# An RWKV-5 layer with a feed-forward part: V loaded and cast by GpSimd's DMA queue, and a new order of steps

## The chip, the cores and the metric

The kernel runs on one core of a Trainium2 chip. The metric is the device time of one execution in microseconds, as the median of several runs. TensorE (PE) multiplies matrices, VectorE (DVE), ScalarE (ACT) and GpSimd (POOL) do elementwise work, SyncE (SP) issues DMAs; SP and GpSimd each have a DMA queue here. Each engine works through its own list of instructions in order and waits on semaphores for what it needs from others.

## The reference

Inputs are `r`, `k`, `v` of shape (4, 8, 768, 48) (batch, heads, time, head size), `w` and `u` of shape (8, 48), and the two matrices `w_in` (384 x 2048) and `w_out` (2048 x 384), all float32.

```python
for t in range(S):
    kt, vt, rt = k[:, :, t], v[:, :, t], r[:, :, t]
    cur = np.einsum('bhd,bhe->bhde', u[None] * kt, vt)
    y[:, :, t] = np.einsum('bhd,bhde->bhe', rt, state + cur)
    state = w[None, :, :, None] * state + np.einsum('bhd,bhe->bhde', kt, vt)
x = y.transpose(0, 2, 1, 3).reshape(B * S, H * D)        # 3072 x 384
h = x @ w_in
g = np.where(h >= 1, h, np.where(h <= -1, 0.0, (h + 1) ** 2 / 4))
return g @ w_out
```

## The kernel before, in words

The recurrence is computed in chunks of 128 time steps. There are six chunks and four batches; a **group** is one chunk of two batches (two **units**), so there are 12 groups, numbered 0 to 11, even ones for batches 0 and 1, odd ones for batches 2 and 3. A group holds 256 tokens.

For each group the kernel does this; the step's name in the order list is in brackets, and `g` stands for the group, `n = 2g + j` for a unit.

- Loads of R, K and V, time on the partitions, 16 heads of 48 values each (`LRg`, `LKg`, `LVg`). One load of a group is 384 KB in runs of 192 bytes. All three are issued on SP's queue. V arrives as float32 in `Vi`, and ScalarE casts it into the bfloat16 tile `Vb` (step `Vg`, L110 by way of the helper `copy`).
- R and K scaled by powers of w, in bfloat16 (`Rsg`, `Ksg`), K times u (`KUg`), R times that (`RKUg`), its sum over each head (`usg`, tile `diag`), and V times that sum (`Bg`, L295). These are products on GpSimd or VectorE; the letter behind "=" says which.
- Rs and Ks turned so that the head size lies on the partitions: by TensorE for the first three groups (`TR`, `TK`, `T`), by transposing DMAs on SP's queue from group 3 on (`RTg`, `KTg`).
- K^T R for each head (`An`, `AAg` for both units), masked to the upper triangle by VectorE (`ATn`). Y is the masked product times V plus the turned R times the state of the chunk before (`Yn`). `yg` adds B. K^T V (`Spn`) updates the state: `Tmg` on VectorE, `decayg` (tile `state`, L398), and a bfloat16 copy by ScalarE (`sbfg`).
- y is turned, by TensorE for groups 0 to 2 (`X`, `xc`), by a transposing DMA on SP's queue from group 3 on (`xcgg`, tile `xT`).
- The feed-forward part in four quarters q of 512 columns: `mg.q` (tile `hp`, 12 matmuls, L457), `rg.q` and `sg.q` on ScalarE (tiles `pt` and `sq`, L468 and L477), `gg.q` on VectorE (L480), `Mg.jq` for the token halves j (tile `op`, 4 matmuls, L492), then a copy out of PSUM (`ogg`) and the store on SP's queue (`stgg`).

The weights are loaded and cast to bfloat16 by DMAs on GpSimd's queue: w_in in three parts (`WI0`, `WI1`, `WI2`), w_out in two (`WO0`, `WO1`). `Zn` are n idle matmuls. Groups 0 and 1 are done by halves: in `LV1.0` the number behind the dot is the unit.

The order of all steps of all engines is one list written out by hand, `ORDER`. The program goes through it word by word, and each engine gets its instructions in that order. `SLOTS` gives the number of buffers of each tile: `Vi` has 3, `Vb` 4.

Of the kernel before, what the change touches and what calls it, by code (L numbers as in the profile page):

```python
# [25 lines left out]
Rs0.0=V WdnS Sp0/0 LK1.0 LK1.1 uS=A KU0.0=V KU0.1=G RKU0.1=G wE TR0/3 cK0=V cR0=A LR1.1 V0.1 wC=V Tm0 Rs0.1=V LV1.0  # L26
LV1.1 RKU0.0=V us0.0 Z16 A0/10 WI0 AT0.0 Ks1.0=G WI1 us0.1 B0.1=G B0.0=V LK2 TR1/2 cR1=A Z21 Sp1/1 AT0.1 Rs1.1=G Tm1
LR2 TK1/3 cK1=A Ks1.1=G TK2/2 Z11 A1/03 AT1.1 Z8 TR3/1 WI2 cR3=A Y0/3 AT1.0 y0 Z7 TK3/1 X0/3 KU1.1=V Rs1.0=V cK3=A
Y1/0 y1 Z14 X1/1 cK2=V V1.0 LK3 RKU1.1=V us1.1 xc0=A xc1=A TR2/2 A3/03 AT3.1 KU1.0=G cR2=A AT3.0 LV2 m0.1/1 r0.1=A
# [11 lines left out]
yg5 M3.03 og3=V xcg5 r4.1 m4.2/3 m4.3/1 g4.0 M4.00/2 M4.10 LK10 Ks7=G RT6 s4.1=A r4.2 LR8 g4.1 M4.01 M4.11 KU7=G  # L41
RKU7=G s4.2=A r4.3 LR10 g4.2 M4.02 M4.12 AA6/30 decayg4=G s4.3=A g4.3 Rs7=G RT7 us7 RKU6=G sbfg4=A m5.1/1 r5.1 M4.03
stg2 AT13 LV10 s5.1=A m5.0/0 r5.0 s5.0=A KU10=G LK8 AT12 KT7 Rs10=G us6 g5.1 M4.13 m5.3/3 Y12/1 Y13 og4=V r5.3 s5.3=A
B6=G g5.0 m5.2/2 r5.2 s5.2=A yg6 xcg6 Rs8=G g5.3 LK9 M5.00/0 Sp10/1 Sp11 M5.01 LR9 V7 Tmg5 decayg5=G M5.10 M5.11 stg4
AA7/31 stg3 g5.2 AT15 V10 m6.1/2 sbfg5=A r6.1 B7=G M5.02 RKU10=G RT8 AT14 m6.0/1 M5.03 m6.3/3 s6.1=A g6.1 KU8=G r6.0
s6.0=A Y14/2 Y15 Ks8=G M5.12 M5.13 r6.3 yg7 m6.2/2 xcg7 g6.0 s6.3=A KT8 og5=A LV11 g6.3 Sp12/1 Sp13 M6.00/0 M6.10
M6.01 M6.11 r6.2 RKU8=G Tmg6 LV8 m7.1/3 s6.2=A g6.2 decayg6=G sbfg6=A Rs9=G us10 AA8/12 r7.1 s7.1=A us8 M6.12 M6.13
LV9 M6.02 AT17 m7.0/2 LK11 AT16 Ks9=G KT9 g7.1 RT9 V8 B8=G Sp14/1 Sp15 M6.03 Tmg7 Y16/3 Y17 yg8 r7.0 s7.0=A m7.2/1
decayg7=G m7.3/3 stg5 Ks10=G r7.2 g7.0 M7.00/2 M7.01 M7.10 M7.11 s7.2=A g7.2 M7.12 xcg8 RT10 og6=V AA9/10 stg6 r7.3
s7.3=A V11 M7.02 LR11 g7.3 M7.03 m8.0/3 M7.13 AT18 KT10 Sp16/1 Sp17 sbfg7=A AT19 KU9=G RKU9=G V9 B10=G KU11=G r8.0  # L50
s8.0=A m8.1/0 us9 B9=G og7=V Y18/2 Y19 Tmg8 decayg8=G stg7 r8.1 s8.1=A g8.0 m8.2/1 m8.3/3 r8.2 Ks11=G yg9 xcg9 M8.00/2
M8.10 g8.1 M8.01 M8.11 s8.2=A Rs11=G KT11 g8.2 m9.0/0 r8.3 s8.3=A M8.12 g8.3 AA10/13 sbfg8=A r9.0 M8.02 M8.03 AT20
M8.13 m9.1/1 RKU11=G s9.0=A AT21 og8=A stg8 Sp18/3 Sp19 Y20/2 Y21 r9.1 s9.1=A g9.0 m9.2/0 RT11 yg10 xcg10 m9.3/2 g9.1
r9.2 M9.00/1 M9.10 M9.11 M9.01 s9.2=A r9.3 s9.3=A Tmg9 m10.0/3 decayg9=G g9.2 M9.02 g9.3 us11 B11=G AA11/20 AT23 M9.12
M9.13 M9.03 m10.1/0 AT22 sbfg9=A r10.0 s10.0=A og9=A stg9 r10.1 Y22/2 Y23 s10.1=A g10.0 M10.00/3 M10.10 m10.2/1 yg11
xcg11 m10.3/2 r10.2 s10.2=A g10.1 M10.11 M10.01 m11.0/0 r10.3 s10.3=A g10.2 M10.02 r11.0 M10.12 m11.1/1 g10.3 M10.03
s11.0=A g11.0 m11.2/2 r11.1 s11.1=A m11.3/0 M10.13 g11.1 M11.00/1 M11.01 r11.2 s11.2=A og10=V r11.3 s11.3=A stg10
M11.10/3 M11.11 g11.2 M11.02 M11.12 g11.3 M11.13 M11.03 o11.1=A st11.1 o11.0=A st11.0
# [14 lines left out]
def kernel(  # L73
# [169 lines left out]
    def do_WO(e, b, i):  # L243
        nc.gpsimd.dma_start(out=w_out_sb[i], in_=w_out_src[:, sum(OUT_PARTS[:i]) * FG : sum(OUT_PARTS[: i + 1]) * FG, :])


    def load(x, what, cls, g, j):
        j0, j1 = by_unit(g, j)
# [1 line left out]
        nc.sync.dma_start(out=t[:, j0 * H : j1 * H, :], in_=source(x, g, j0, j1))  # L250
# [309 lines left out]
```

## Time and profile before

| | |
|---|---|
| median of 3 runs | 182.53 us (180.95 to 185.12) |
| the profiled execution | 181.74 us, of which the span from the first to the last instruction is 180.0 us |
| mean granted TensorE clock | 0.991 |
| busy: TensorE, VectorE, ScalarE, GpSimd | 166.0, 134.7, 126.1, 114.5 us |
| first matmul of the feed-forward part | 20.01 us after the start of the span |
| last matmul ends, last store issued | about 176.4 us |
| DMA packets | 107,191, of which 100,898 are under 512 bytes |

The busy share of an engine is an average over the span; which engine sets the end is read from the stretch in question and from the wait that ends last there. In rows of the profile, a line such as "L110 ACT CAST Vb<-Vi 128x768 bf16<-128x768 f32 x10" names the line of the program, the engine, the operation, the output and input tiles with their shapes and types, and the count; behind the bar stand the total and mean time, and then the idle time of the engine before these instructions with what ended it. "SPq" is an issue on SP's queue. Queue q1 is SP's, q0 GpSimd's.

### The profile page before, as it was taken

How to read it: one execution, taken by the hardware profiler on the slowest of the kernel's cores; microseconds unless marked ns; L12 is line 12 of the kernel's file. 1: busy time of each engine (PE TensorE's matmuls, PEld its weight loads, DVE VectorE, ACT ScalarE, POOL GpSimd, SP SyncE). 2: the span in 40 equal slices, each digit the busy share in tenths (PEclk: the TensorE clock that was granted, in tenths of full speed). 3: DMA queues.
4: the chain of work that ended last, by engine and by line, in shares of the span. 5: the costliest groups of instructions: out<-in, count | busy, mean ns of one | idle time of the engine just before them, and what ended most of it. 6: DMA issues, size and time to landing. Idle time of an engine off the chain costs nothing.

```text
span 180.0 us, 4051 instructions
## 1 busy us (share of the span) xinstructions
PE 166.0 (92%) x1678; PEld 125.7 (70%) x1678; DVE 134.7 (75%) x156; ACT 126.1 (70%) x144; POOL 114.5 (64%) x82
## 2 busy tenths in 40 slices
...
GB/s 113 192 181 207 224 184 198 206 211 173 152 185 181 222 166 206 182 169 190 197 153 238 176 252 181 179 169 221 241 192 135 12 146 44 4 133 0 5 87 87
DMA packets 107191, 28.78 MB, mean 160 GB/s; under 512 B 100898, under 2 KB 106788, under 8 KB 107172
## 3 DMA queue, kind: packets, MB, share of 16 engines
q1 hardware_dynamic: 103888, 25.37, 80.0%
...
q14 instruction: 6, 0.05, 0.1%
q10 hardware_dynamic: 4, 0.00, 0.0%
...
## 4 chain that ended last, share of the span: by engine, by line
PE 65%; DMA 19%; DVE 5%; POOL 3%; SPq 3%; ACT 2%; issue 1%; DVEq 0%
PE op L492 29%; PE hp L457 28%; DMA w_out<-in_moe_w_out_dram 6%; DMA w_in<-in_moe_w_in_dram 4%; DMA xT<-y 4%; SPq L250 3%; DMA Ki<-in_k_dram 3%; DVE g L480 2%; PE A L352 2%; DMA out_dram<-o 2%; PE Y L420 2%; PE Y L414 2%; DVE y L432 2%; POOL Ks L264 2%; PE Sp L387 1%
## 5 line engine op out<-in xcount | busy, mean ns | idle before, releaser
L457 PE MATMUL hp<-xT,w_in 128*128 128x256 bf16 x576 | 70.5, 275 | 5.5 <-DMA xT<-y 3.6
L480 DVE SCALAR_TENSOR_TENSOR g<-sq,hp 128x1024 bf16<-128x1024 bf16 x48 | 58.2, 1217 | 17.4 <-ACT sq L477 17.1
L492 PE MATMUL op<-w_out,g 128*128 128x384 bf16 x384 | 69.0, 326 | 1.5 <-DMA w_out<-in_moe_w_out_dram 1.5
L457 PEld LDWEIGHTS <-w_in 128*128 128x128 bf16 x576 | 55.8, 98 | 16.2 <-DMA xT<-y 4.0
L468 ACT ACTIVATE pt<-hp 128x1024 f32<-128x1024 f32 x47 | 47.8, 1017 | 23.4 <-PE hp L457 23.3
L492 PEld LDWEIGHTS <-g 128*128 128x128 bf16 x384 | 36.2, 98 | 22.8 <-issue 1.4
L477 ACT ACTIVATE sq<-pt 128x1024 bf16<-128x1024 f32 x47 | 49.7, 1057 | 1.4
L295 POOL TENSOR_TENSOR V<-Vb,diag 128x768 f32<-128x768 bf16 (+1 forms) x13 | 17.3, 1329 | 16.0 <-ACT Vb L110 10.6
L361 DVE TENSOR_TENSOR AT<-A,umask 128x1024 bf16<-128x1024 f32 x20 | 23.6, 1218 | 3.5 <-PE A L352 3.5
L264 POOL TENSOR_TENSOR KU<-Ki,u_sb 128x768 f32<-128x768 f32 (+1 forms) x12 | 21.0, 1750 | 5.4 <-ACT u_sb L110 5.2
L398 POOL TENSOR_TENSOR state<-Tm,wCm 128x768 f32<-128x768 f32 x8 | 14.5, 1817 | 11.8 <-DVE Tm L395 11.8
L264 POOL TENSOR_TENSOR Ks<-Ki,Wdn 128x768 bf16<-128x768 f32 (+1 forms) x12 | 20.2, 1682 | 1.5 <-DMA Ki<-in_k_dram 1.5
L264 POOL TENSOR_TENSOR RKU<-Ri,KU 128x768 f32<-128x768 f32 (+1 forms) x12 | 20.3, 1696 | 0.7 <-DMA Ri<-in_r_dram 0.3
L264 POOL TENSOR_TENSOR Rs<-Ri,Wup 128x768 bf16<-128x768 f32 (+1 forms) x10 | 17.4, 1739 | 4.8 <-DMA Ri<-in_r_dram 4.8
L432 DVE TENSOR_TENSOR y<-Y,V 128x768 bf16<-128x768 f32 x10 | 9.6, 956 | 9.4 <-POOL KU L264 5.0
L110 ACT CAST state_bf<-state 128x768 bf16<-128x768 f32 (+1 forms) x12 | 8.6, 716 | 4.4 <-POOL state L398 4.4
L286 DVE TENSOR_REDUCE diag<-RKU 128x16 f32<-128x768 f32 (+1 forms) x14 | 11.6, 831 | 0.1
L110 ACT CAST Vb<-Vi 128x768 bf16<-128x768 f32 (+1 forms) x14 | 10.1, 734 | 1.8 <-DMA Vi<-in_v_dram 1.8
L420 PE MATMUL Y<-Vb,AT 128*128 128x48 bf16 x192 | 10.4, 187 | 0.7 <-ACT Vb L110 0.7
L110 ACT COPY o<-op 128x768 f32<-128x768 f32 (+1 forms) x7 | 4.9, 703 | 8.0 <-PE op L492 8.0
L420 PEld LDWEIGHTS <-AT 128*128 128x128 bf16 x192 | 9.6, 99 | 1.1 <-issue 0.9
L519 PE MATMUL z<-idle 128*128 128x128 bf16 x96 | 8.3, 253 | 1.2 <-DVE idle L132 1.2
...
## 6 DMA issues: line engine op xcount, KB each, us to landing
...
w_out<-in_moe_w_out_dram POOLq DMA_DIRECT2D x2, 768.0 KB, 9.5
...
```

Of the source, the lines that this page charges most:

```text
L110: nc.scalar.copy(out, in_) if e == "A" else engines[e].tensor_copy(out, in_)
L264: engines[e].tensor_mul(part(out)[:, :, :, :D], part(a), rep(b, j1 - j0) if len(b.shape) == 3 and b.shape[1] == H else part(b))
L295: engines[e].tensor_mul(t[:, hs, :], tiles["V", g][:, hs, :], tiles["diag", g][:, hs].unsqueeze(2).to_broadcast([P, n, D]))
L361: nc.vector.tensor_mul(t.rearrange("p i n t -> p (i n) t"), tiles["A", n].rearrange("p i (n t) -> p (i n) t", t=P), umask.unsqueeze(1).to_ ...
L398: engines[e].tensor_mul(states[g % BP], tiles["Tm", g], flat(wCm).unsqueeze(1).to_broadcast([P, UNITS, DM]))
L420: nc.tensor.matmul(Y[:, h * D : (h + 1) * D], AT[:, i, p, :], V[:, j * H + h, :], start=(c == 0), stop=True, skip_group_check=True,)
L432: nc.vector.tensor_add(y, tiles["Y", "of", g][:, :, :DM], flat(tiles["V2", g]).rearrange("p (j d) -> p j d", j=UNITS))
L457: nc.tensor.matmul(hp[:, f, :], w_in_sb[wi][:, i, (wo * FG + f) * P : (wo * FG + f + 1) * P], tiles["xT", g][:, :, i, :], start=(i == 0), ...
L468: nc.scalar.activation(t, tiles["hp", g, q], AF.Relu, bias=0.5, scale=0.5)
L477: nc.scalar.activation(t, p, AF.Square)
L480: nc.vector.scalar_tensor_tensor(out=make("g", ("g", g, q), [P, FG, TOK], BF16), in0=tiles["sq", g, q], scalar=1.0, in1=tiles["hp", g, q], ...
L492: nc.tensor.matmul(tiles[key][:, k, :DO], tiles["g", g, q][:, f, j * P : (j + 1) * P], w_out_sb[wi][:, wo * FG + f, :], start=(q == 0 and ...
```

## The change

`LVg` no longer loads float32 on SP's queue. It issues a DMA on GpSimd's queue that writes bfloat16 straight into `Vb`. The switch `CAST_FROM` is 0, so this holds for every group. The steps `Vg` are gone from the list, and the whole list is laid out anew. Some products move between GpSimd and VectorE: RKU2, RKU3, B3 and decay2 go to VectorE, and among the half steps of groups 0 and 1 some go each way.

```diff
 ORDER = """
-Zs/0 LV0.0 LK0.0 LK0.1 LR0.0 ln Z19 bw/0 V0.0 LV0.1 bu/1 LR0.1 Wdn/2 Ks0.1=V wq/3 WupS Ks0.0=V TK0/2 LR1.0 Wup/1
...
-s0.0=A sbf0=A g0.0 xc2=V Sp3/0 r0.2=A X3/1 xc3=V LR3 WO0 sbf1=A m0.3/0 Ks2=G s0.2=A Tm3 r0.3=A s0.3=A Rs2=G WO1 m1.1/2
...
-Y6/2 g2.0 KU4=G RKU4=G s2.1=A Y7 yg3 r2.2=A m2.3/1 RT4 M2.00/2 g2.1 Sp4/3 KU5=G s2.2=A r2.3=A s2.3=A xcg3 LR5 Sp5
...
-s3.0=A r3.1 s3.1=A M2.13 M2.03 LK6 g3.0 og2=A B4=G m3.2/3 Tmg3 LR6 RT5 sbfg2=A r3.2 s3.2=A LV5 AA4/20 g3.1 LK7 RKU5=G
-M3.00/1 M3.01 AT9 AT8 m3.3/0 Y8/2 g3.2 Ks6=G V6 Y9 yg4 xcg4 r3.3 M3.10 M3.11 s3.3=A AA5/32 us5 LR7 M3.02 KT6 M3.12
-g3.3 KU6=G decayg3=G sbfg3=A Rs6=G V5 AT11 Sp8/0 Sp9 M3.13 B5=G m4.0/2 stg1 AT10 Y10/3 Y11 Tmg4 LV7 m4.1/0 r4.0 s4.0=A
...
+Zs/0 LR0.0 LK1.0 ln LK0.0 LV0.0 Z20 bw/1 LK0.1 LV0.1 LR0.1 LV1.0 LR1.0 bu/3 WdnS Ks1.0=G WupS Wdn/0 uS=A wq/2 Wup/1
+LR1.1 Ks0.0=V KU0.0=V wE Ks0.1=V KU0.1=G wC=A LK1.1 Z7 TK1/1 TK0/3 cK1=A LV1.1 Rs0.1=V Z6 TR1/2 RKU0.0=V us0.0 LR2 WI0
+cR1=A Rs0.0=V LK2 Z17 TR0/1 LK3 A1/02 RKU0.1=V Rs1.0=G cR0=V cK0=V us0.1 AT1.1 B0.0=G Z14 Sp2/1 Z2 A0/23 Tm2 WI1
...
+AT3.1 AT2.0 us1.0 Sp3/3 AT3.0 B1.0=G r0.1=A m0.0/0 us1.1 WO0 s0.1=A Sp0/2 B1.1=G Y2/1 Tm0 g0.1 Y3/2 r0.0=A y2 m0.3/1
+s0.0=A y3 X3/0 r0.3=A s0.3=A g0.0 LR4 Ks2=G X2/2 xc2=V xc3=V m0.2/0 Tm3 g0.3 r0.2=A m1.1/2 m1.0/3 WO1 Rs2=V s0.2=A
...
+xc5=V us3 B3=V AA3/02 LV4 og1=A m2.0/1 RT4 sbf3=A AT6 KU4=G m2.1/3 sbf2=A r2.0=A s2.0=A Ks4=G AT7 m2.2/0 LK6 r2.1=A
+g2.0 s2.1=A Y6/2 Y7 M2.00/1 yg3 RKU4=G r2.2=A M2.10 g2.1 xcg3 m2.3/2 s2.2=A KU5=G KT4 M2.01 g2.2 r2.3=A Sp4/3 LR5 Sp5
+M2.11 M2.12 Ks5=G Tmg2 s2.3=A us4 LR6 LR7 m3.0/0 g2.3 KU6=G m3.1/3 r3.0 LV5 Sp6/2 decayg2=V Sp7 M2.13 s3.0=A LK7 M2.02
+r3.1 Tmg3 B4=G M2.03 KT5 s3.1=A g3.0 m3.2/2 Rs5=G og2=A g3.1 AA4/01 sbfg2=A decayg3=G r3.2 AT9 RT5 s3.2=A m3.3/3 AT8
+M3.00/1 LV6 g3.2 r3.3 M3.10 Rs6=G Y8/0 Y9 s3.3=A M3.11 yg4 sbfg3=A M3.12 Ks6=G g3.3 xcg4 M3.01 RKU5=G M3.02 stg1 Sp8/2
+Sp9 Tmg4 KT6 AA5/03 M3.13 m4.0/2 AT11 LK9 KU7=G LK8 AT10 M3.03 r4.0 og3=V m4.1/3 s4.0=A RT6 us5 m4.2/0 g4.0 B5=G r4.1
+Y10/1 Y11 s4.1=A m4.3/2 RKU6=G r4.2 yg5 M4.00/1 xcg5 s4.2=A g4.1 M4.10 RKU7=G r4.3 LK10 LR8 M4.01 g4.2 M4.11 M4.02
+s4.3=A us6 stg2 decayg4=G g4.3 m5.0/0 us7 B6=G sbfg4=A AA6/32 AT13 M4.12 LR10 M4.03 r5.0 s5.0=A KU8=G AT12 m5.1/2
...
+g5.3 xcg6 Sp10/0 Sp11 M5.10 s5.2=A Tmg5 M5.11 LK11 LV7 M5.01 decayg5=G g5.2 AA7/30 LR9 M5.12 AT15 m6.0/1 sbfg5=A
+RKU8=G AT14 M5.02 r6.0 m6.1/0 Ks8=G s6.0=A M5.13 r6.1 g6.0 KT8 M5.03 KU10=G m6.3/3 s6.1=A og5=V LR11 B7=G g6.1 Y14/1
+Y15 r6.3 RT8 m6.2/2 KU9=G yg7 s6.3=A r6.2 Sp12/0 Sp13 xcg7 g6.3 M6.00/1 M6.10 LV8 s6.2=A stg4 Tmg6 M6.11 g6.2 M6.01
...
 """
 
 SLOTS = {..., "Vi": 3, "Vb": 4, ...}
+CAST_FROM = 0
...
     def do_LV(e, b, g, j=None):
-        load(v, "V32", "Vi", g, j)
+        if g < CAST_FROM:
+            load(v, "V32", "Vi", g, j)
+        else:
+            j0, j1 = by_unit(g, j)
+            t = make("Vb", ("V", g), [P, UNITS * H, D], BF16)
+            nc.gpsimd.dma_start(out=t[:, j0 * H : j1 * H, :], in_=source(v, g, j0, j1))
```

More of the change, by code (lines that the diff above doesn't have):

```diff
@@ L24 @@
 ORDER = """
-Zs/0 LV0.0 LK0.0 LK0.1 LR0.0 ln Z19 bw/0 V0.0 LV0.1 bu/1 LR0.1 Wdn/2 Ks0.1=V wq/3 WupS Ks0.0=V TK0/2 LR1.0 Wup/1
[L26 to L29, printed above, removed]
@@ L40 @@
-g3.3 KU6=G decayg3=G sbfg3=A Rs6=G V5 AT11 Sp8/0 Sp9 M3.13 B5=G m4.0/2 stg1 AT10 Y10/3 Y11 Tmg4 LV7 m4.1/0 r4.0 s4.0=A
[L41 to L58, printed above, removed]
+Zs/0 LR0.0 LK1.0 ln LK0.0 LV0.0 Z20 bw/1 LK0.1 LV0.1 LR0.1 LV1.0 LR1.0 bu/3 WdnS Ks1.0=G WupS Wdn/0 uS=A wq/2 Wup/1
@@ new lines @@
+s0.0=A y3 X3/0 r0.3=A s0.3=A g0.0 LR4 Ks2=G X2/2 xc2=V xc3=V m0.2/0 Tm3 g0.3 r0.2=A m1.1/2 m1.0/3 WO1 Rs2=V s0.2=A
+KU2=G g0.2 m1.2/1 r1.1=A r1.0=V s1.1=A s1.0=A M0.00/0 M0.10 KU3=G g1.1 M0.11 g1.0 r1.2=A M0.01 T5/2 s1.2=A LV2 M1.00/3
+c5=V Ks3=G M1.10 g1.2 LV3 M1.01 A5/2 T4/1 AT5 KT3 M1.11 c4=A RKU2=V M0.02 sbf0=A A4/1 m1.3/2 Rs3=G us2 B2=G AT4 M0.12
+r1.3=A RKU3=V M0.13 RT3 M0.03 M1.02 s1.3=A og0=A LK4 g1.3 Y4/1 LK5 Y5 M1.12 Rs4=G yg2 M1.03 stg0 X4/2 X5/1 M1.13 xc4=A
+xc5=V us3 B3=V AA3/02 LV4 og1=A m2.0/1 RT4 sbf3=A AT6 KU4=G m2.1/3 sbf2=A r2.0=A s2.0=A Ks4=G AT7 m2.2/0 LK6 r2.1=A
```

21 lines of the change are left out of this document (15 added, 6 removed).

## The prediction

> **What bounds the kernel now.** I read the busy shares first, then stretches of 10 us, then the chain of the work that ended last, then the waits.
>
> ```profile
> PE 166.0 (92%) x1678; PEld 125.7 (70%) x1678; DVE 134.7 (75%) x156; ACT 126.1 (70%) x144; POOL 114.5 (64%) x82
> ```
>
> TensorE is busy for 92% of the span of 180 us; no other engine is above 75%. An engine that is relieved therefore gives time back only where TensorE stands idle and waits for it. The stretches say where that is; their columns are the stretch, its length, and the busy time of PE, PEld, DVE, ACT and POOL with the instructions in brackets, then the granted clock, the share of the DMA engines and GB/s.
>
> ```profile
> 20.00:30.00 10.00, 8.57 (x99) 7.36 (x100) 9.03 (x15) 8.62 (x12) 6.69 (x6) 1.00 1.10 197
> 30.00:40.00 10.00, 8.34 (x79) 6.06 (x77) 7.86 (x9) 7.59 (x9) 7.53 (x5) 1.00 1.27 204
> ...
> 70.00:80.00 10.00, 6.42 (x75) 4.28 (x72) 6.64 (x7) 3.51 (x4) 10.00 (x7) 0.97 1.34 173
> 80.00:90.00 10.00, 10.00 (x87) 7.64 (x86) 5.67 (x6) 8.41 (x9) 9.78 (x6) 0.86 0.99 206
> ...
> 150.00:160.00 10.00, 10.00 (x105) 7.26 (x103) 7.96 (x8) 7.38 (x8) 2.83 (x2) 1.00 0.12 42
> ```
>
> Two places lose time once the feed-forward part has begun. Between 20 and 40 TensorE is idle for 1.43 + 1.66 = 3.1 us, between 70 and 80 for 3.6 us. After the second gap the granted clock is lower (0.97, then 0.86), which costs another 0.03 x 10 + 0.14 x 10 = 1.7 us. A late stretch is full: nothing is to be won there. The chain (start, length, what) and the waits (total, times, longest) name the causes.
>
> ```profile
> 12.22 7.74 DMA w_in<-in_moe_w_in_dram
> ...
> 46.16 0.05 PE Y L414
> 46.20 0.05 PE Y L420 x2
> ...
> 59.61 0.34 PE Sp L387 x8
> 59.95 1.31 PE hp L457 x12
> 61.26 0.65 PE op L492 x4
> ...
> 66.48 0.55 PE A L352 x16
> ...
> 71.72 6.66 DMA xT<-y
> ```
>
> ```profile
> PE hp L457 <- DMA xT<-y: 3.6, 1, 3.6
> ...
> PE op L492 <- DMA w_out<-in_moe_w_out_dram: 1.5, 2, 1.3
> ...
> PE Y L420 <- ACT Vb L110: 0.7, 1, 0.7
> ```
>
> The rows of TensorE in the chain are also my prices for its steps: 1.31 for an m, 0.65 for an M, 0.55 for an AA, 0.34 for a pair of Sp, and about 0.37 for a Y (four times a state matmul and two of V). The 3.6 us are one wait, for the transposing DMA of group 4's y (step xcg4), which took 6.66 us from its issue to its landing. Of the early 3.1 us, 1.5 are waits for w_out and 0.7 one for a cast of V; the rest is scattered. xT mostly lands sooner, and SP's queue shows why it did not here (the first row is xT's, then queue q1, then one issue on SP):
>
> ```profile
> DMA to landing us min/median/max: 2.7/2.8/6.7
> ```
>
> ```profile
> q1 hardware_dynamic: 103888, 25.37, 80.0%
> ```
>
> ```profile
> 31.45 6.65 SPq L250 DMA_DIRECT2D Vi<-in_v_dram  x1
> ```
>
> SP's queue q1 holds the DMA engines for 80.0% of the span, and SP sits up to 6.65 us on the issue of one load of V: the transfers are backed up there. xcg4 comes right behind five issues on that queue (LK6, LR6, RT5, LV5, LK7), one of them V's, four of them whole loads.
>
> **The change, part by part.** It removes 14 casts on ScalarE, takes 14 loads off SP's queue, puts 14 DMAs into GpSimd's list, and re-orders everything.
>
> ```profile
> L110 ACT CAST Vb<-Vi 128x768 bf16<-128x768 f32 (+1 forms) x14 | 10.1, 734 | 1.8 <-DMA Vi<-in_v_dram 1.8
> ```
>
> (a) **ScalarE** loses 10.1 us. TensorE is the bound, so this counts only in the early gaps, where the wait of Y for Vb (0.7) goes. There WO1 also comes sooner: behind WO0 the old list has Ks2 and Rs2, the new one half a B and Ks2, and GpSimd no longer waits for casts before them. I take 0.8 of the 1.5 us of w_out back. Together -1.5; bounds 0 and -3.1, all that is idle there.
>
> (b) **SP's queue** loses a third of its loads, so xT has less ahead of it. In the new order xcg4 follows two transposing DMAs and, before these, loads of K and R alone. What covers it on TensorE until m4.0 are three M, one AA and a pair of Sp: 3 x 0.65 + 0.55 + 0.34 = 2.8 us, as long as the median landing. So the gap and its clock go: -3.6 - 1.7 = -5.3. But the cover is thinner than before (five M, one AA, a pair of Sp: 4.1 us), and at xcg5 it is four M, 2.6 us, with LK9, LK8 and RT6 ahead on the queue. I add +1.2 for new waits on xT; bounds 0, and 6.7 - 2.6 = 4.1 for one bad landing.
>
> The page "DMA: Bandwidth & Descriptors" of the Trainium skill, section "Issuing engines are not separate DMA queues", speaks against this gain: transfers that different engines start run on the same 16 DMA engines and interleave, and a second issuer saves only issue time. By that rule the -5.3 is luck of the order, and the wait may come back anywhere: rival 1 is what that would make of the time. The share of 1.34 in the stretch of the wait agrees that the DMA engines are full; no row of before has V on the other queue.
>
> (c) **GpSimd** gets the 14 issues.
>
> ```profile
> L295 POOL TENSOR_TENSOR V<-Vb,diag 128x768 f32<-128x768 bf16 x10 | 14.8, 1477 | 11.9 <-ACT Vb L110 9.3 <-DVE diag L286 2.6
> L398 POOL TENSOR_TENSOR state<-Tm,wCm 128x768 f32<-128x768 f32 x8 | 14.5, 1817 | 11.8 <-DVE Tm L395 11.8
> ...
> L241 POOL DMA_DIRECT2D w_in<-in_moe_w_in_dram x3 | 2.5, 845 | 0.0
> ...
> L244 POOL DMA_DIRECT2D w_out<-in_moe_w_out_dram x2 | 1.9, 939 | 0.0
> ...
> L264 DVE TENSOR_TENSOR Rs<-Ri,Wup 128x768 bf16<-128x768 f32 x1 | 0.9, 949 | 0.0
> ```
>
> By their tiles, w_in's issue has 128 x 3 = 384 runs of memory, w_out's 128 x 8 = 1024; V has 128 x 16 = 2048 runs of 192 bytes for a group, 1024 for a half. Bounds for a group: 0.85 us if runs cost nothing, 2 x 0.94 = 1.88 if they cost in proportion to w_out's. The two rows rise by 0.09 us over 640 runs, so 1024 more cost 0.15; with a margin I take 1.15, and 0.94 for a half: 10 x 1.15 + 4 x 0.94 = 15.3 us more. In return RKU2, RKU3, decayg2 and B3 go to VectorE: -3 x 1.82 - 1.48 = -6.9. On VectorE these are four steps of about 0.95, 3.8 us on an engine that is 75% busy, hidden under TensorE (if that cover fails, 3.8 at most, before 60 us). GpSimd ends near 114.5 + 15.3 - 6.9 = 123 us. But from LV4 to LV7 its list holds 19 products of 1.82, three B of 1.48 and three issues: 42.5 us, and TensorE's list between the same words (16 m, 27 M, 3 AA, 8 Y, 4 pairs of Sp) is 44.5. GpSimd is 95% full there, and a late B or Ks stops TensorE through yg or KT. At 1.15 it fits; at 1.88 it slips by 3 x 0.73 - 2.0, about nothing. Later (LV7 to B11) it is 46.3 of 51.5.
>
> (d) **V's landing** becomes a direct wait of Y and Sp on TensorE and of B on GpSimd, where Ks, KU, Rs and decay queue behind a waiting B, and KT, RT and the state behind them. The lead on TensorE's list is 19 us for LV4, but for LV7 (to Y14) 7.7, LV8 (to Y16) 8.4, LV9 (to Y18) 8.7 and LV10 (to Y20) 5.9. Landings before, V's on SP and w_out's on GpSimd:
>
> ```profile
> DMA to landing us min/median/max: 3.1/7.0/12.2
> ```
>
> ```profile
> w_out<-in_moe_w_out_dram POOLq DMA_DIRECT2D x2, 768.0 KB, 9.5
> ```
>
> Ends are 3.1 and 12.2. I take 6.5: V's median, a little less since no load of K and R stands ahead of it on its queue. Then only a short wait is left; for (c) and (d) together I put +1.0, bounds 0 and the 10 of rival 2.
>
> The same page of the Trainium skill, section "Anatomy of one DMA — SWDGE (gpsimd) path", has a fit of 2.0 us plus bytes over 436 GB/s, an estimate of 3.8 us for the 0.79 MB of a w_out part. The trace has 9.5, so the fit is not used; by it the +1.0 would be 0.
>
> (e) **The start.** The chain runs through w_in's second part, issued at 12.22 and landed 7.74 later. In the new list GpSimd issues LV0.0, LV0.1 and LV1.0, does two halves of products, issues LV1.1 and then WI0; V's four halves go ahead of w_in on one queue. I put +0.5 for the first hp; bounds 0 and 2. A wait of LV for a free buffer costs nothing: with four buffers, the old content is that of four groups earlier, long read.
>
> Sum: -1.5 - 5.3 + 1.2 + 1.0 + 0.5 = -4.1. The profiled execution took 181.74 us, so 177.6; it lies 0.8 below the median of the three runs (182.53), so for a median I say **178.4 us**, 2.3% below that. About 2% (3.7 us) is what a measurement of this kernel can tell from no change.
>
> **The rivals.**
> 1. The transfers stay backed up and a wait for xT returns, at xcg5 or xcg3: the +1.2 becomes 4.1 plus half the clock's loss, 5.0, and the sum 182.2. For it: the share of 1.34, the same bytes to read, the thin covers. Against: V leaves the queue on which xT waits, and the median xT landed in 2.8. Chance 0.28.
> 2. V lands late and the kernel gets slower. Place: Y14, Y16, Y18, Y20. It decides from a landing of 7.7 us on; at 10.5 the shortfalls are 2.8 + 2.1 + 1.8 + 4.6 = 11.3, the last one less because few loads run that late (share 0.12 after 150): some 8. With 1.7 of lost clock, in place of the +1.0, this gives 187. For it: w_out's 9.5 on the same queue, and V's short runs. Against: V's 7.0 on the fuller queue, half the bytes written. Chance 0.19.
> 3. The early 3.1 us go wholly, and no wait for xT or V comes: 178.4 - 1.6 - 1.2 - 1.0 = 174.6. Chance 0.08.
> 4. GpSimd's issues cost 1.88 us or more, its list is the bound in the middle and VectorE's extra steps show: three us, 181.4. Chance 0.05.
>
> That the change doesn't do what it says is no rival: no step V is left in the list.
>
> **How the numbers follow.** The forecast has 0.40; its own range is 175 to 181 (the bounds of (a), (b) and (e), partly against each other), and a little of it lies above the bound of 178.9. Faster by over 2%: 0.36 of the forecast and the 0.08 of rival 3, so 0.44. Slower: rival 2 without its mild end, 0.18. Within 2%: the rest, 0.38. From 174.5 to 187 the range leaves out the far half of rival 2 and some of rival 3.
>
> **What the profile after would show.** ScalarE near 116 us and GpSimd near 123, with issues of about 1.15 us; V's packets on q0 and as many fewer on q1; no wait of hp for xT above 2 us and a clock of 1.00 between 70 and 90; V's landing below 7.7 us and no wait of Y or Sp for it; the first hp at 20 to 21 us. I am wrong if Y waits for the DMA of Vb, if a wait of 3 us for xT stands anywhere, or if an issue of V holds GpSimd for 2 us or more.

## The result, and the profile after

The changed kernel takes 191.46 us (median of 4 runs, 189.66 to 192.89); the kernel before took 183.82 us beside it (4 runs, 180.95 to 186.89). The ratio is 1.048 with a 95% interval of 1.040 to 1.057: slower, where 178.4 us was forecast. Ratios leave out the executions that ran slower at a lower granted clock, and where only one other is left (e1, e4, e7), that one is compared, as "one run", without a ratio.

The page of the changed kernel, its part on busy time:

```profile
PE 168.3 (89%) x1677; PEld 128.0 (68%) x1677; DVE 144.7 (76%) x155; ACT 119.3 (63%) x134; POOL 123.6 (65%) x93
```

GpSimd came out as worked out beforehand and ScalarE 3 us above; VectorE did not: it rose by 10.0 us (144.7 - 134.7) where 3.8 were expected. The first matmul of the feed-forward part and its last one (line hp of the view by tile, kernel before, then after; the times are starts) split the difference of the profiled executions (191.33 - 181.74 = 9.6 us):

```profile
L457 PE MATMUL hp<-xT,w_in x576: 269/273/417, 20.0 to 170.2; 128*128 128x256 bf16 x192
```

```profile
L463 PE MATMUL hp<-xT,w_in x576: 269/273/418, 24.7 to 180.5; 128*128 128x256 bf16 x192
```

The start takes 4.7 us longer, the way from the first hp to the last 155.8 instead of 150.2 us (+5.6), and the tail to the end of the span 0.7 us less. The stretches and TensorE's waits of the changed kernel, in the columns explained in the prediction:

```profile
20.00:30.00 10.00, 8.42 (x111) 7.17 (x109) 7.59 (x15) 6.43 (x10) 3.59 (x5) 0.83 0.97 171
30.00:40.00 10.00, 9.22 (x79) 7.32 (x78) 9.35 (x12) 7.68 (x9) 9.93 (x8) 1.00 1.29 191
50.00:60.00 10.00, 6.02 (x73) 4.43 (x70) 9.31 (x6) 6.15 (x8) 8.94 (x6) 1.00 0.99 138
60.00:70.00 10.00, 9.03 (x81) 6.75 (x81) 7.99 (x8) 4.16 (x4) 1.55 (x1) 0.83 0.24 50
70.00:80.00 10.00, 10.00 (x115) 7.83 (x114) 9.66 (x9) 8.86 (x10) 9.96 (x8) 1.00 1.47 175
80.00:90.00 10.00, 7.01 (x69) 5.08 (x68) 6.13 (x6) 2.64 (x4) 6.58 (x4) 1.00 1.24 198
```

```profile
PE hp L463 <- DVE AT L367: 5.0, 1, 5.0
PE A L358 <- DMA RT<-Rs: 3.0, 1, 3.0
PE hp L463 <- DMA xT<-y: 2.8, 3, 1.3
PE Sp L393 <- DVE AT L372: 2.0, 1, 2.0
```

The wait of 3.6 us for xT is gone, as is the gap at 70 to 80. In its place TensorE idles for 4.0 us between 50 and 60, with a clock of 0.83 behind it (60 to 70), and for 3.0 between 80 and 90. From 20 to 30 the clock is 0.83 too. The largest wait is now for a mask product of VectorE (AT). VectorE is busy for 9.31 of these 10 us with 6 instructions: one of them must be long. Its timeline (start, length) and GpSimd's:

```profile
52.40 0.94 DVE L292 TENSOR_REDUCE diag<-RKU 128x16 f32<-128x768 f32 x1
53.38 6.40 DVE L301 TENSOR_TENSOR V<-Vb,diag 128x768 f32<-128x768 bf16 x1
59.71 1.21 DVE L367 TENSOR_TENSOR AT<-A,umask 128x1024 bf16<-128x1024 f32 x1
```

```profile
50.63 1.20 POOL L265 DMA_DIRECT2D Vb<-in_v_dram  x1
51.86 1.83 POOL L270 TENSOR_TENSOR KU<-Ki,u_sb 128x768 f32<-128x768 f32 x1
53.63 1.82 POOL L270 TENSOR_TENSOR Ks<-Ki,Wdn 128x768 bf16<-128x768 f32 x1
55.40 1.81 POOL L270 TENSOR_TENSOR RKU<-Ri,KU 128x768 f32<-128x768 f32 x1
57.16 1.80 POOL L270 TENSOR_TENSOR KU<-Ki,u_sb 128x768 f32<-128x768 f32 x1
```

This is B3, one of the four products that the change gives to VectorE. It was priced at 0.95 us and holds VectorE for 6.40. It ends at 59.78, 0.82 us after GpSimd's row of four products ends (57.16 + 1.80 = 58.96): it looks as if it had stood still through that row and had then run at its usual pace. Behind it in VectorE's list wait AT6 and AT7, behind these Y and the states, and GpSimd in turn:

```profile
68.45 1.83 POOL L270 TENSOR_TENSOR Ks<-Ki,Wdn 128x768 bf16<-128x768 f32 x1 [9.49 <-PE Sp L393]
```

GpSimd is idle for 9.5 us in the part of its list that the prediction had called 95% full. In the start VectorE's Ks1.1 (0.56 us where it is undisturbed, in e4 below) is stretched beside GpSimd in the same way:

```profile
15.46 2.46 DVE L270 TENSOR_TENSOR Ks<-Ki,Wdn 128x384 bf16<-128x384 f32 x1
```

```profile
15.40 0.84 POOL L301 TENSOR_TENSOR V<-Vb,diag 128x384 f32<-128x384 bf16 x1
16.19 1.00 POOL L270 TENSOR_TENSOR KU<-Ki,u_sb 128x384 f32<-128x384 f32 x1
17.13 0.80 POOL L242 DMA_DIRECT2D w_in<-in_moe_w_in_dram  x1
```

Ks1.1 ends at 17.92; AT1.0 and AT0.0 stand behind it, and TensorE's wait of 2.0 us for AT (above) follows.

### The profile page after: what moved, and what is told of

Read it like the earlier page. It is cut to its first block, busy times and chain, and to the rows that moved or that the text cites. A ratio compares the mean times of both kernels' runs of the same rounds, so it can differ in the third digit from the quotient of the medians.

```text
span 189.6 us, 4045 instructions
## 1 busy us (share of the span) xinstructions
PE 168.3 (89%) x1677; PEld 128.0 (68%) x1677; DVE 144.7 (76%) x155; ACT 119.3 (63%) x134; POOL 123.6 (65%) x93
## 3 DMA queue, kind: packets, MB, share of 16 engines
q1 hardware_dynamic: 79088, 20.65, 58.3%
q0 software_dynamic: 28080, 5.51, 35.3%
## 4 chain that ended last, share of the span: by engine, by line
PE 43%; DVE 14%; issue 14%; POOL 13%; DMA 11%; ACT 2%; SPq 1%; DVEq 0%; POOLq 0%; ACTq 0%
PE hp L463 17%; PE op L498 16%; DMA xT<-y 8%; DVE g L486 4%; POOL KU L270 4%; DMA out_dram<-o 3%; PE z L525 3%; POOL Rs L270 2%; POOL V L301 2%; POOL RKU L270 2%; POOL Vb L265 2%; DVE y L438 2%; DVE Ks L270 1%; PE Y L426 1%; DVE AT L372 1%
## 5 line engine op out<-in xcount | busy, mean ns | idle before, releaser
L367 DVE TENSOR_TENSOR AT<-A,umask 128x1024 bf16<-128x1024 f32 x20 | 23.8, 1218 | 3.6 <-PE A L358 3.5
L270 POOL TENSOR_TENSOR Ks<-Ki,Wdn 128x768 bf16<-128x768 f32 (+1 forms) x11 | 19.2, 1743 | 10.2 <-PE Sp L393 9.5
L270 POOL TENSOR_TENSOR Rs<-Ri,Wup 128x768 bf16<-128x768 f32 (+1 forms) x11 | 19.1, 1734 | 1.0 <-DMA Ri<-in_r_dram 0.9
L404 POOL TENSOR_TENSOR state<-Tm,wCm 128x768 f32<-128x768 f32 x7 | 12.7, 1809 | 9.6 <-DVE Tm L401 9.6
L265 POOL DMA_DIRECT2D Vb<-in_v_dram x14 | 15.7, 1125 | 0.0
L270 POOL TENSOR_TENSOR RKU<-Ri,KU 128x768 f32<-128x768 f32 (+1 forms) x9 | 15.4, 1721 | 0.2
L525 PE MATMUL z<-idle 128*128 128x128 bf16 x95 | 10.6, 279 | 1.2 <-DVE idle L133 1.2
L426 PE MATMUL Y<-Vb,AT 128*128 128x48 bf16 x192 | 10.6, 188 | 0.5 <-DVE state L397 0.5
L401 DVE TENSOR_TENSOR Tm<-Sp,state 128x768 f32<-128x768 f32 x8 | 7.6, 956 | 2.5 <-PE Sp L393 1.5
```

What stands on the lines that cost most here:

```text
L265: nc.gpsimd.dma_start(out=t[:, j0 * H : j1 * H, :], in_=source(v, g, j0, j1))
L270: engines[e].tensor_mul(part(out)[:, :, :, :D], part(a), rep(b, j1 - j0) if len(b.shape) == 3 and b.shape[1] == H else part(b))
L367: nc.vector.tensor_mul(t.rearrange("p i n t -> p (i n) t"), tiles["A", n].rearrange("p i (n t) -> p (i n) t", t=P), umask.unsqueeze(1).to_ ...
L426: nc.tensor.matmul(Y[:, h * D : (h + 1) * D], AT[:, i, p, :], V[:, j * H + h, :], start=(c == 0), stop=True, skip_group_check=True,)
L525: nc.tensor.matmul(tiles["z"][:, 0, :P], idle[:, :P], idle[:, :P], start=True, stop=True)
```

## The experiments

**Theory 1:** a VectorE product with both inputs in SBUF cannot run while GpSimd reads SBUF, and the change puts such products beside GpSimd's rows. The page "SBUF — State Buffer" of the Trainium skill, section "SBUF: two separate sides", has this rule: a VectorE instruction with two inputs in SBUF and a GpSimd instruction that reads SBUF need the same pair of ports, and the one that starts first has it for the whole instruction. The run m1 below agrees as far as one instruction goes: beside GpSimd's products VectorE's product took 1.94 us with two inputs in SBUF and 0.89 with one in PSUM. **Rivals:** V's DMA itself costs (rival 2 of the prediction), GpSimd's list is too long, or the order is bad for another reason. All diffs are words of `ORDER` unless said otherwise.

**B3 back on GpSimd (e1).**

```diff
-B3=V
+B3=G
```

> One letter of the changed kernel: B3=V becomes B3=G. Theory 1 (a product with both inputs in SBUF on VectorE can't run beside GpSimd's products: B3 took 6.40 us on VectorE and ended 0.95 us after GpSimd's row of four went idle): B3 takes 1.5 us on GpSimd, the wait of hp for AT (5.0 us), the lower clock after it (0.83 for 10 us, 1.7 us) and the 9.5 us wait of GpSimd's Ks for Sp go; GpSimd gets 1.5 us more. Time 183 to 186, ratio to before 1.00 to 1.015. Theory 2 (V's DMAs in GpSimd's list and their landing are the cause): stays at 190 to 192, ratio about 1.05. Theory 3 (GpSimd's list is simply too long): 191 to 193, as GpSimd gets 1.5 us more.

183.79 us (one run; the median of all four is 187.67). It is the profiled execution, and it has 150.2 us from the first hp to the last, as before the change and 5.6 less than the changed kernel. The long wait is gone and its price with it; other products on VectorE stay stretched (decay2 took 3.15 us). The first hp came at 22.9 us, 1.8 sooner than in the changed kernel, though the words of the start are the same: Ks1.1 was asked for before GpSimd's B had begun, and came in ahead of it.

```profile
15.23 0.83 DVE L270 TENSOR_TENSOR Ks<-Ki,Wdn 128x384 bf16<-128x384 f32 x1
```

**All six such products on GpSimd (e2).**

```diff
-Ks1.1=V  Rs2=V  RKU2=V  RKU3=V  B3=V  decayg2=V
+Ks1.1=G  Rs2=G  RKU2=G  RKU3=G  B3=G  decayg2=G
```

> The changed kernel with six two-input products back from VectorE to GpSimd: B3, Rs2, RKU2, RKU3, decayg2 and the half Ks1.1. GpSimd gets 1.5 + 4 x 1.8 + 1.0 = 9.7 us more, VectorE loses 6.4 + 2.0 + 0.95 + 1.3 + 1.6 + 2.5 = 14.8 us by the trace of the changed kernel. Theory 1 (the shared port): the first hp comes about 2 us sooner (Ks1.1 took 2.46 us instead of 0.55), no VectorE product above 1.5 us behind it, time 182 to 186. Theory 3 (GpSimd's list is the bound): 190 to 194, with waits of VectorE's y and of the transposes for GpSimd. Theory 2 (V's DMAs): 190 to 192.

184.10 us (183.51 to 185.94), 1.010 times the kernel before (1.001 to 1.019), where the changed kernel has 1.048. Six words take 7.4 us off by medians, though GpSimd is busy for 132.6 us instead of 123.6: a GpSimd list that is too long isn't what made the change slow.

**V's DMA alone, in the old order (e3), and the new order alone (e4).** In e3 the old list keeps its order, but for LV1.0 and LV1.1, which go up behind LV0.1; the steps V go, V's loads go to GpSimd's queue. In e4 the new list has V's loads on SP and the casts on ScalarE, both at places that I chose.

```diff
 # e3: ORDER of before
-V0.0 V0.1 V1.0 V1.1 V2 ... V11
-"Vb": 4      CAST of V on ScalarE
+"Vb": 7      CAST_FROM = 0
 # e4: ORDER of after, V0.0 ... V11 put in ahead of their uses,
 #     LV2 ... LV11 (but LV4) moved
+CAST_FROM = 12
```

> The DMA part alone: the order of before, the steps V gone, V cast by its own DMA on GpSimd's queue at the old places of LV (only LV1.0 and LV1.1 go up behind LV0.1), seven buffers of Vb. Theory 1: V's DMA does no harm: 178 to 183, ratio 0.97 to 1.00, V lands in 4 to 9 us, and the wait of hp for xT of 3.6 us shrinks, as SP's queue carries less. Theory 2: 187 to 192, with waits for V or a slower GpSimd. Rival 1 of the prediction (the transfers stay backed up): 181 to 184 with the wait for xT as before.

> The order alone: the new order with V loaded as float32 on SP's queue and cast on ScalarE just ahead of its first use (from group 5 on the load stands 5 us of TensorE's work further ahead, since three buffers of Vi and a cast come between). Theory 1 (the products that the new order puts on VectorE): B3 again takes 3 us or more on VectorE, hp waits for AT, time 187 to 192, ratio 1.03 to 1.05. Theory 2 (V's DMAs): 180 to 184, ratio about 1.00.

e3: 189.2 us, ratio 1.035 (1.028 to 1.042): a miss, since theory 1 left it at 178 to 183. e4: 188.46 us (one run; the median of all four is 193.17). So V's DMA costs by itself in the old order, and the new order costs by itself too, by that one run. B3 took only 1.67 us in e4, beside the same closed row of GpSimd products, which theory 1 as it stood could not say. Another product was held there, Rs2. It stands beside a row of GpSimd that has the issue of a DMA for w_out ahead of it, and ends 0.83 us after that row (37.14 and 36.31):

```profile
33.64 3.50 DVE L270 TENSOR_TENSOR Rs<-Ri,Wup 128x768 bf16<-128x768 f32 x1
```

```profile
29.98 0.94 POOL L245 DMA_DIRECT2D w_out<-in_moe_w_out_dram  x1
30.94 3.60 POOL L270 TENSOR_TENSOR KU<-Ki,u_sb 128x768 f32<-128x768 f32 x2
34.50 1.81 POOL L270 TENSOR_TENSOR Ks<-Ki,Wdn 128x768 bf16<-128x768 f32 x1
```

**B3 on VectorE in the kernel before (e5).**

```diff
 # ORDER of before
-B3=G
+B3=V
```

> The kernel before with one letter changed: B3=G becomes B3=V, nothing else. Behind B3 GpSimd's list there has Rs4, KU4, RKU4, KU5 and Ks5. Theory 1 (a VectorE product with both inputs in SBUF gets in only when GpSimd has no such product queued): B3 takes 3 to 8 us on VectorE instead of 0.95, the masks AT7 and AT6 behind it are late, hp waits; time 186 to 190, ratio 1.01 to 1.03, although GpSimd is 1.5 us shorter. Theory 2 (V's DMAs alone are the cause; they aren't in this kernel): B3 takes 0.95 to 1.5 us and the time stays at 183 to 184.

184.76 us, ratio 1.007 (0.998 to 1.016), and B3 took 0.95 us. A miss: it ran in a pause of 0.98 us, in which GpSimd waited for a load. The pair of engines alone does not decide. No load of V is issued by GpSimd in this kernel.

**LV4 moved into the row (e6).** GpSimd's order becomes KU4, Ks4, LV4, RKU4, KU5.

```diff
-LV4 og1=A m2.0/1 ... Ks4=G
+og1=A m2.0/1 ... Ks4=G LV4
```

> The changed kernel with one word moved: LV4 goes from ahead of KU4 to behind Ks4 in GpSimd's list, so a DMA issue of 1.2 us, which reads no tile in SBUF, stands in the middle of the row beside B3=V. Theory 1: B3 gets in during that issue (as Rs2 did during LV2 in the changed kernel), takes 1 to 3 us instead of 6.4, the 5.0 us wait of hp for AT shrinks to under 2; time 185 to 188. If a waiting VectorE product just has to wait for the whole stretch until GpSimd waits for a semaphore, B3 stays at 6 us and the time at 190 to 192. Theory 2 (V's DMAs): no change, 190 to 192.

B3 took 1.66 us and the kernel 185.38 (ratio 1.011, 1.001 to 1.022): one word gives 6 us by medians. This agrees with theory 1, but it changes two things: the row gets a gap, and it loses the DMA issue ahead of it.

**The ports by themselves (m1, m2).** m1 runs rows of GpSimd products beside VectorE products, in stages kept apart; m2 goes through forms, buffers, waits and the moment of the request.

```diff
+fence(); G(6); red(1); two(2)    # m1: GpSimd a*b six times; VectorE a reduction, then a*b twice
+fence(); G(4); red(1); psum(4)   # m1: one input of VectorE's product in PSUM
+fence(); G(4); red(4)            # m1: reductions, one input
+fence(); forms(); red(); B()     # m2: GpSimd KU, Ks, RKU, KU as in the kernel; VectorE B
```

> This kernel computes nothing of the reference; it runs products of 128x768 float32 on GpSimd and VectorE beside each other, in stages kept apart by small copies. Theory (a VectorE instruction with two inputs in SBUF can't run while GpSimd reads SBUF, and comes in only when GpSimd's queue has a gap): alone a VectorE product takes 0.95 us and a GpSimd one 1.8 us. Beside a row of six GpSimd products, the first VectorE product with two SBUF inputs, started about 1 us into the row, lasts until the row ends, some 10 us, the second 0.95 us; with one input in bfloat16 the same. With one input in PSUM, or as a reduction of one input, it takes 0.95 us beside a row of four. Where GpSimd's row is broken by DMA issues, each break lets VectorE in, so no product lasts over about 2.8 us. When VectorE's row of twelve starts together with GpSimd's four, one side waits for the other. Rival (the two merely share a bandwidth): each product beside GpSimd's lasts about twice as long, 1.9 us, and none 10 us.

> This kernel computes nothing of the reference; ten stages kept apart by small copies, each with a row of four products on GpSimd and one VectorE product with two SBUF inputs asked for about 1 us into the row. Theory 1 (the form decides: the kernel's own forms with broadcast inputs and separate buffers run back to back on GpSimd without letting VectorE in): stages 1, 2, 5, 6 let VectorE in after one GpSimd product (it lasts about 1.9 us, the next GpSimd product 2.5), stages 3, 4 and 8 hold it until the row ends (5 us and more). Theory 2 (the moment decides: asked for in the last 0.5 us of a GpSimd product, VectorE misses its turn): stages 7 and 8 hold it, 1 to 6 let it in. Theory 3 (separate buffers decide): stages 2 and on hold it, stage 1 alone lets it in. In stage 10 the product asked for during the DMA issue waits for the next GpSimd product.

m1, VectorE's rows with one input in PSUM and with one input in all, and GpSimd's row beside the first:

```profile
46.61 3.54 DVE L80 TENSOR_TENSOR dv<-pt,a 128x768 f32<-128x768 f32 x4
...
53.48 3.90 DVE L84 TENSOR_REDUCE rd<-a 128x16 f32<-128x768 f32 x4
```

```profile
45.94 7.09 POOL L68 TENSOR_TENSOR pg<-a,b 128x768 f32<-128x768 f32 x4
```

Both run at their pace (0.89 and 0.98 us each), and so does GpSimd (1.77). But beside a row of six GpSimd products the two-input product lasted 1.94 us, not 10: it came in after the product then running, and the next GpSimd product took 2.52. The expected 10 us were a miss. Where GpSimd had a DMA issue behind each product, VectorE's products that stood behind an issue lasted 3.04 to 3.19 us (2.8 at most were expected): they waited for one GpSimd product and came in at the next issue. In m2 the forms, the buffers and the moment changed nothing (1.69 to 2.55 us in stages 1 to 9). Only in the last stage, with a DMA issue inside GpSimd's row, was an instruction, a copy asked for during the issue, held through two products, for 4.34 us. All three theories of m2 fell, and that stage gave the next one.

**A DMA issue ahead of the row (m3).**

```diff
+fence(); issue(); row(4); reds(3); mul()   # 1: DMA issue on GpSimd, four products; VectorE asks in the first
+fence(); row(4); reds(2); mul()            # 2: the same without the issue
```

> This kernel computes nothing of the reference; eight stages, each with a row of four GpSimd products and one VectorE product with two SBUF inputs. Theory (behind a DMA issue, GpSimd's row of products lets nothing in until it ends or meets a wait): in stages 1, 3 and 4 (issue, then four products; asked for in the first product, during the issue, in the second product) the VectorE product ends 0.8 to 0.9 us after the row's last GpSimd product, so it lasts 4 to 8 us, and no GpSimd product lasts over 1.9 us. In stage 2 (no issue) and 5 (the DMA issued by SyncE) it comes in after one GpSimd product, and the next takes 2.5 us. In stage 7 (a wait for ScalarE after two products) it comes in at that wait. Stages 6 (a small copy between issue and row) and 8 (a memset in the row) show whether anything else ends the hold. Rival (the moment of the request decides, not the issue): stages 1 and 4 let it in after the product that is running, and only 3 does not.

Stage 1, VectorE's product and GpSimd's row, then stage 2, in the same views:

```profile
14.51 6.66 DVE L93 TENSOR_TENSOR dv<-a,b 128x768 f32<-128x768 f32 x1
...
23.39 0.96 DVE L93 TENSOR_TENSOR dv<-a,b 128x768 f32<-128x768 f32 x1
```

```profile
13.27 7.07 POOL L75 TENSOR_TENSOR pg<-a,b 128x768 f32<-128x768 f32 x4
...
21.72 7.79 POOL L75 TENSOR_TENSOR pg<-a,b 128x768 f32<-128x768 f32 x4
```

With the issue ahead, the product ends 0.83 us after the row's end (21.17 and 20.34), and GpSimd's row isn't stretched. Without it the product comes in at the next end of a GpSimd product, and the row is 0.7 us longer. Asked for during the issue it lasts 8.55 us, in the second product 5.59; a small copy behind the issue changes nothing (6.69), nor does a memset in the row (5.50, to its end). A DMA issued by SyncE does no harm (0.96). A wait for ScalarE after the second product lets VectorE in there (3.07). The rival, the moment of the request, is out. The transfer behind the issue is not what holds VectorE: in the stage of 8.55 us the product ended at 39.50, and from 35.5 on the DMA engines moved nothing (share 0.00). SyncE's DMA was a plain float32 load, though, so the issuer and the kind of load changed together there.

**The same in the kernel (e16).** LV4 goes ahead of B2, for which GpSimd waits anyway; the row KU4, Ks4, RKU4, KU5 has neither an issue ahead nor a gap.

```diff
-B2=G ... LV4 og1=A
+LV4 B2=G ... og1=A
```

> The changed kernel with one word moved: LV4, the issue of V's DMA for group 4, stands ahead of B2 (for which GpSimd waits some 8 us) instead of ahead of KU4. The row KU4, Ks4, RKU4, KU5 on GpSimd is then as closed as in the changed kernel, but no DMA issue stands ahead of it. Theory (an issue makes the row behind it hold VectorE off, and a wait ends that): B3 comes in after one product, 1.7 us instead of 6.4, one GpSimd product takes 2.5 us, and the time is 184 to 187 us, as with the issue inside the row (185.4). Rival (a closed row holds VectorE off in any case): B3 takes 6 us or more, and the time stays at 190 to 192 us.

B3 and GpSimd's row in this run:

```profile
53.31 1.67 DVE L301 TENSOR_TENSOR V<-Vb,diag 128x768 f32<-128x768 bf16 x1
```

```profile
52.34 1.82 POOL L270 TENSOR_TENSOR Ks<-Ki,Wdn 128x768 bf16<-128x768 f32 x1
54.13 2.53 POOL L270 TENSOR_TENSOR RKU<-Ri,KU 128x768 f32<-128x768 f32 x1
56.62 1.82 POOL L270 TENSOR_TENSOR KU<-Ki,u_sb 128x768 f32<-128x768 f32 x1
```

The row is as closed as in the changed kernel, and B3 now comes in after one product; RKU4 pays 0.7 us for it. 185.60 us (184.47 to 186.85), ratio 1.011 (0.999 to 1.023) where the changed kernel has 1.048: 5.9 us by medians, from the position of one word. The closed row alone is out as the cause. It also explains e4: there no issue stood ahead of B3's row, and one stood ahead of Rs2's.

The rule has exceptions among the half products of the start. Ks1.1, with the same words around it and an issue ahead of GpSimd's row, was held through two products up to the next issue in the changed kernel, e6 and e16 (2.46, 2.19 and 2.36 us), but came in after one in e1 (0.83). What tells these apart is open.

**What the rest of the change is worth.** The new order with V on SP and the six words (e9), the new order with V's DMA from group 2 on (e8), and seven words with V's DMA (e10):

```diff
 # e8: e2, groups 0 and 1 by SP and ScalarE: V0.0 ... V1.1 put in,
 #     LV0.0, LV0.1 and LV1.1 moved
+CAST_FROM = 2
 # e9: e4, and the six words of e2
 # e10: e2, and
-RKU1.1=V
+RKU1.1=G
```

> e2 (the new order with the six products back on GpSimd) with the V of groups 0 and 1 loaded on SP's queue behind the halves of K and R that are needed first, and cast on ScalarE; DMA cast from group 2 on. Theory A: the first hp comes at 20 to 21.5 us instead of 22.5, time 181 to 183.5. Theory B: 184 as e2, since the length of GpSimd's list is what counts; it gets 3.6 us shorter in the start, so at most 1 us less.

> The new order with V loaded on SP and cast on ScalarE (as in the run of the order alone, 193.2 us), and six VectorE products with two SBUF inputs given to GpSimd. Theory (the loss sits in those products, V's DMA is worth next to nothing by itself): 183 to 187 us, first hp at 22 to 23 us and about 151 us from the first hp to the last, as the same six words gave with V's DMA (184.1 us). Rival (V's DMA pays, the new order without it does not): 188 us or more. Rival (V's DMA still costs): under 182 us.

> The changed kernel with the six products on GpSimd and one more, RKU1.1, which took 1.35 us instead of 0.55 beside GpSimd's row and stands ahead of y1 in VectorE's list. Theory: first hp 0.5 to 1 us earlier than 22.5, the rest as it was (150.5), so 183 to 184 us against 184.1; the kernel before at 183 to 185, so a ratio of 0.995 to 1.005. Rival (the start is set by other things): first hp stays at 22.5.

e8: 188.79 us, ratio 1.026 (1.012 to 1.040), a miss; the first hp came at 25.4. e9: 188.54 us, ratio 1.023 (1.013 to 1.032). Its theory missed and its first rival held: against e4's one run (188.46) the six words bring nothing there. With V's DMA the same list takes 184.1 (e2, ratio 1.010): in this order V's DMA is worth some 1.3%, by the ratios, against SP's loads at the places that I chose. e10: 184.46 us, ratio 1.001 (0.996 to 1.007), first hp at 21.3: the changed kernel without the conflicts is as fast as the one before, no faster. Among its waits of TensorE:

```profile
PE hp L463 <- DMA xT<-y: 4.9, 4, 1.9
PE A L358 <- DMA RT<-Rs: 2.5, 1, 2.5
```

That is 7.4 us for transposing DMAs on SP's queue, where the kernel before had 3.6. They are not the whole reason: e2 is as fast with 3.3 us of them, and waits 2.6 us for VectorE's Tm instead.

**Why V's DMA costs in the old order.** e7 keeps SP and ScalarE for groups 0 and 1, e11 and its repeat e14 for groups 6 to 11, e15 for groups 3 to 11; e13 repeats e3.

```diff
 # ORDER of before, with the steps V of these groups alone
-        if g < CAST_FROM:
+        if g >= SP_FROM:      # e11, e14: 6; e15: 3 (e7: CAST_FROM = 2)
```

> The order of before; the V of groups 0 and 1 as before (SP's queue, cast on ScalarE), V cast by its own DMA on GpSimd's queue from group 2 on. The run with all groups so (e3) lost 3.8 us up to the first hp (23.8 against 20.0) and showed a clock of 0.72 from 20 to 30. Theory A (in the start V's four halves on a queue of their own take about 40% of the packets from K's and R's halves, which the start waits for): the first hp at 20 to 21 us, clock 1.00, time 180 to 184, ratio 0.98 to 1.00. Theory B (GpSimd's longer list is what costs e3 its 3.5%): 187 to 190.

> The old order with V's DMA on GpSimd for groups 0 to 5 alone; groups 6 to 11 are loaded on SP and cast on ScalarE as before. The old order with all twelve gave 189.2 us, with first hp at 23.8 and 152.9 us from there to the last hp. Theory A (the start costs 3.8 us of that, the filled list of GpSimd at 60 to 100 us the other 2.7): first hp stays at 23 to 24 us, the rest comes back to 150 to 151, so 186 to 187 us. Theory B (all of it is the start's low clock and port waits): as the run with all twelve, 189 us. Theory C (each group's DMA costs its part): 186 us with first hp at 22.

> The old order with V's DMA on GpSimd for all twelve groups, once more (189.2 us then, first hp at 23.8). If its loss lies in the late groups, it stays 4 to 6 us above the run with six groups on the same chip, and the profile shows 152 to 154 us from the first hp to the last; if it was the start's luck, it comes to 183 to 186 us with first hp at 20 to 22.

> The old order with V's DMA for groups 0 to 5 alone, once more (183.3 us then, ratio 0.993 to before). If that was no luck of the start, 182.5 to 184 us again and a ratio of 0.985 to 0.998; if it was, 185 to 188 us with first hp at 22 to 24.

> The old order with V's DMA on GpSimd for groups 0 to 2 alone, the others on SP and ScalarE as before. Theory (GpSimd's list is free before about 60 us and full after it, so each issue costs only where the list is full): 182.5 to 184.5 us, as with six groups (183.3 and 184.1), first hp at 20 to 22, 150 to 151 us from there. Rival (groups 3 to 5 cost their part as well): 181 to 182.5 us, and a ratio to before below 0.99.

With all twelve groups 188.5 us (e13, ratio 1.030, 1.020 to 1.040); with the first six 183.26 (e11, 0.993, 0.987 to 0.999) and 184.09 (e14, 0.999, 0.993 to 1.004). So the first six groups' DMAs cost nothing that can be seen and the last six 4 us by medians. The start does not tell them apart: in e3 and e13, the same program, it came out at 23.8 and 20.6. Three stretches of e13, then of e14:

```profile
100.00:110.00 10.00, 9.35 (x95) 6.99 (x92) 8.59 (x9) 7.06 (x8) 7.26 (x6) 1.00 1.08 189
110.00:120.00 10.00, 8.89 (x92) 6.68 (x90) 7.84 (x8) 6.81 (x8) 9.96 (x7) 1.00 1.09 154
120.00:130.00 10.00, 8.65 (x90) 6.07 (x91) 5.65 (x6) 4.35 (x5) 7.11 (x5) 0.83 1.47 166
```

```profile
100.00:110.00 10.00, 9.77 (x102) 7.35 (x101) 7.79 (x8) 8.38 (x10) 7.88 (x5) 1.00 1.15 222
110.00:120.00 10.00, 10.00 (x104) 7.09 (x101) 8.74 (x9) 7.65 (x9) 8.80 (x6) 1.00 0.95 168
120.00:130.00 10.00, 10.00 (x112) 7.47 (x110) 8.16 (x9) 8.34 (x10) 8.28 (x6) 1.00 1.11 210
```

TensorE loses 0.42 + 1.11 + 1.35 = 2.9 us here, and 1.7 by the clock. Between 60 and 100, GpSimd is busy for 39.8 of 40 us in e13 and for 37.4 in e14, and V's slowest landing is alike (11.7 and 11.8). That GpSimd's filled list is the cause fits, but no run took that alone away. A rival is untested: the transposing DMAs themselves land later in e13 (KT after 6.3 us in the median, 4.5 in e14), and TensorE's one longer wait for a DMA in these three stretches is 2.5 us for KT. The hold is not the difference: Rs3 on VectorE lasts 3.23 us in e13 and 3.32 in e14. e7 gave 189.02 us (one run; the median of all four is 193.80), over its 180 to 184 and beside e13, so keeping groups 0 and 1 on SP did not help. e15 gave 187.02 us with an interval of 0.974 to 1.052, which says nothing.

## Why the prediction was wrong

**The step that failed is in (c):** "four steps of about 0.95, 3.8 us on an engine that is 75% busy, hidden under TensorE (if that cover fails, 3.8 at most, before 60 us)". The price was the row of a lone product. Which engine's reads it would run beside wasn't asked, and neither was what an issue of V does to GpSimd's row. B3 alone took 6.40 us, and what waited behind it was AT, on TensorE's path. The cap of 3.8 us was a sum of busy times, and B3 alone went 5.45 us over its part of it. No rival named this. Rival 4 came nearest, with "VectorE's extra steps show", but it had them from issues of 1.88 us and for three us; the slow side was given to V's landing. e2 prices the step at 7.4 us by medians, e16 the hold on B3 at 5.9. The six words of e2 include Ks1.1 and Rs2, which the prediction did not price; Rs2 goes to VectorE in exchange for Rs3, which the description of the change leaves out.

**(e), the start:** +0.5 with bounds 0 and 2 was mis-sized; it was +4.7. Ks1.1 held for 2.46 us is a part of it: with Ks1.1 at 0.83 the first hp came at 22.9 (e1), without it and the five others at 22.5 (e2), with RKU1.1 moved too at 21.3 (e10). Since the old order's start came out between 20.6 and 23.8 with one program, the rest can't be told from its spread.

**(b), the transfers:** -5.3 + 1.2 was right in what it named and wrong in what it summed. The gap at 70 to 80 closed and hp's longest wait for xT was 1.3 us. But it did not ask what is late next once xT is in time. That was RT: TensorE waits 3.0 us for it, and 5.8 us in all for transposing DMAs against 3.6. In e10, without the seven products, it is 7.4. The queues after:

```profile
q1 hardware_dynamic: 79088, 20.65, 58.3%
q0 software_dynamic: 28080, 5.51, 35.3%
```

SP's queue holds the DMA engines for 58.3% instead of 80.0%, and GpSimd's for 35.3: the packets are the same 107,191. The page "DMA: Bandwidth & Descriptors" of the Trainium skill, section "Issuing engines are not separate DMA queues", says that transfers of different issuers share the same engines; the trace agrees, as the two queues hold 93.6% together against 90.6 before (80.0 and 10.6). Rival 1 was nearer to the truth of this part than the forecast. The waits of 1.5 us for w_out and 0.7 for a cast (a) did go, the first wholly where 0.8 was counted.

**Right:** GpSimd's issues, and V's landing (d).

```profile
L265 POOL DMA_DIRECT2D Vb<-in_v_dram x14 | 15.7, 1125 | 0.0
```

```profile
DMA to landing us min/median/max: 4.3/6.6/8.4
```

15.7 us against 15.3, GpSimd busy for 123.6 against 123, the landing's median 6.6 against 6.5. TensorE waits for no V, so rival 2 did not come, and no issue cost 1.88 us, the condition of rival 4.
